# Column-tiled image transposes, a new order of weight loads and a new instruction order in a memory-recurrent attention kernel

## Chip, cores and metric

The kernel runs on one NeuronCore of a Trainium2 chip. The metric is device time of one execution in microseconds (us); several executions are timed, and one of them is profiled. All runs told here are of the ordinary ("fast") state, with a mean granted TensorE clock of 0.98 to 0.99. A ratio of two kernels is the mean time of one's fast runs over the mean of the other's fast runs of the same rounds on the same chip, so it isn't quite the ratio of the medians quoted beside it.

## The reference

Four layers alternate over 2048 tokens of width 512: A, B, A, B. Layer A is attention with a recurrent memory and decides the structure. Tokens come in 64 segments of 32; each segment is attended together with 8 memory rows, and the first 8 output rows become the memory of the next segment.

```python
for s in range(n_seg):                       # 64 segments, one after another
    xs = x[:, s * seg_len:(s + 1) * seg_len, :]
    h = jnp.concatenate([mem, xs], axis=1)   # 8 + 32 rows
    q = jnp.einsum('btd,dhe->bhte', h, Wq)   # 32 heads of 128; k and v likewise
    ...
    p = _softmax(jnp.where(mask, q @ k.T * scale, -1e9))
    o = jnp.einsum('bhte,hed->btd', p @ v, Wo)
    mem = o[:, :M, :]                        # the chain from segment to segment
    outs.append(o[:, M:, :])
```

Layer B is a linear attention over all tokens; its work is spread as filler over the segments of layer A. Wq, Wk, Wv and Wo have 4 MB each and stay in on-chip memory.

## The kernel before

The kernel is a list of nodes (a few instructions each, with the data they read and write) that a program orders on five engines before the launch. Each node has a priority: its step in the kernel plus a searched offset. Three parts matter here.

The loads of the weights. Nodes with smaller step plus offset go first; 13.5 is the length of a step, so with the old offsets Wv (-15.85) overtook Wk (4.75) and Wk overtook Wq (20.70), although the estimated landings belong to the order Wq, Wk, Wv:

```python
for i, (W, v, nm, t) in enumerate(((Wq_sb, qk_view[0], "Wq", 12.0), (Wk_sb, qk_view[1], "Wk", 21.0),
                                   (Wv_sb, qk_view[2], "Wv", 30.3))):
    P.at(-998 + i, "ld%d" % (2 + i))
    late.append(add("act", lambda a, W=W, v=v: a.dma_start(W[:, :, :], v), 0.5, writes=[nm], ..., lat=t))
# ... Wo: four quarters on SyncE; each waits for the load before the previous one
for i in range(4):
    nd = add("sp", lambda s, hs=hs: s.dma_start(Wo_sb[:, hs, :], ...), 0.9, ..., after=[late[-2]], ...)
    late.append(nd)
```

A projection of 32 rows fills only 32 columns of TensorE's array, so four of them run side by side in column tiles (`mode="col"`). The result, an "image", is copied out of PSUM (the memory that TensorE writes to) and, for queries and keys, must be turned. Of 640 images 256 are turned on TensorE and 384 by a DMA transpose. The latter are half of the images of each segment and all those of the "left blocks" (a segment has 40 rows; the 8 that do not fit into a block of 32 are gathered from four segments):

```python
def turned(W, key, blk, bkeys, b, dst, dkey, urgent, dma):
    tl = project(W, key, blk, bkeys, b, urgent)          # L753, mode="col"
    k = img_no[0] % NI if urgent else NI                  # one of few image buffers
    nd = evac(img[:, k, :], lambda: tl.f32()[:, :], 512, ..., writes=[("img", k)])   # L591 or L592
    if dma:
        add("sp", lambda e: e.dma_start_transpose(..., img[:, k, :]), 1.25, reads=[("img", k)], ...)   # L766
        return nd
    def tr(pe):                                           # L773
        for i in range(4):
            r = pe.transpose(tt.bf16()[:, 128 * i:128 * i + 128], img[:, k, 128 * i:128 * i + 128], id_sb[:, :])
        return r
    add("pe", tr, c_pe(4, 128), reads=[("img", k), "id"], tiles=[tt], urgent=urgent)   # mode "full"
    evac(dst..., 512, ...)
```

The ordering stays in the mode that TensorE is in (full array or column tiles) unless a node of the other mode is ahead by more than `MODE_SLACK` (`LOOK` is how far ahead, in us, it looks for a more urgent node before it fills in another):

```python
elif nd.prio < pick.prio - MODE_SLACK:
    break                       # the other mode is far more urgent: change
elif nd.mode == self.pe_mode:
    pick = nd                   # stay
```

Lines that the profiles name: L753 projections, L773 image transposes, L834 memory scores (L851, L864, L865: their sums and products), L889 and L800 scores in column tiles, L925 and L926 products with V, L949 output projection, L972 the hand-over of the memory to the next segment, L990 residual, L1085 and above layer B. In the changed kernel L773 is L775, and all lines below it are 3 higher (L834 is L837, L949 is L952, L972 is L975).

The softmax here doesn't subtract the row's maximum and nothing guards it: scores larger than these inputs give would overflow.

Of the kernel before, what the change touches and what calls it, by code (L numbers as in the profile page):

```python
# [16 lines left out]
HOP = 0.06  # L17
PE_SWITCH = 0.1
TURN = 1.8
MODE_SLACK = 26.39  # L20

LOOK = 0.000

PERIOD = 13.5
OFFSET = {
    "ld0": (-11.50,),
    "ld1": (4.90,),
    "ld2": (20.70,),
    "ld3": (4.75,),
    "ld4": (-15.85,),  # L30
    "startF": (-5.20,),
    "prepF": (4.30, 1.75, -2.15, 3.05, 7.55, 4.10, 2.90, -8.85, -8.80, 12.20, 4.50),
    "left0F": (-3.40, 1.15, -4.60, -5.90, 5.70, 0.00),
    "left1F": (-4.60, 1.35, -0.70, -0.35, 1.15, 5.25),
    "leftv0F": (30.85, -17.50),
    "leftv1F": (2.10, -15.75),
    "leftsF": (-4.25, 3.65, -1.55, 9.80),
    "xl": (16.05,),
    "qk0": (-19.20, -4.30, -2.55, -8.90, -4.20, 0.30),
    "qk1": (-1.75, 2.40, -4.40, 2.35, -6.40, -9.20, 11.50, -0.15),  # L40
    "v0": (0.30, 8.50),
    "v1": (4.55, 0.65),
    "mem0": (5.45, -0.45, -1.20, 0.55, 0.20, -2.10, 0.00, 1.25, -1.35),
    "mem1": (-10.80, -25.05, -8.05, 0.00, -0.65, -10.60, -14.15, 3.00, 0.60),
    "out": (-6.35, -2.55, -6.45, -3.20),
    "next": (0.50, -3.60, 0.10),
    "x": (3.45, 13.20, 11.25, -10.75, 6.60, -2.75, 26.25, -5.65, -0.15, -7.90, -8.10, -6.15, 7.95, -1.90,
        -5.05, -1.85, 6.35, 27.05, 19.50, 11.50, 27.45, 16.35, -0.50),
    "res": (28.65, 17.45, -1.00, -9.55, -0.60, -2.20, 2.25),
    "prep": (0.00, 11.35, 2.65, 5.95, -0.35, -1.00, 0.00, -3.10, 0.25, 1.85, -0.05),  # L50
    "left0": (3.25, -0.60, -3.40, -9.65, -2.20, 1.05),
    "left1": (34.80, -0.50, 7.70, 40.15, 13.10, -6.25),
    "leftv0": (0.00, 1.50),
    "leftv1": (42.50, 4.65),
    "lefts": (6.45, 0.40, 7.15, -4.05),
    "bi": (1.50, 4.25, -14.35, -1.70, 12.10, -1.15, -0.10, -3.45, 0.35, 17.45, 17.75, 0.10, 9.80, 16.90, 15.05,
        17.50, 7.80, 0.05, 0.60, -0.55, 4.90, -5.05, 5.75),
    "xL": (12.95, 3.75, 2.20, 1.30, -2.00, -0.25, -0.40, 8.00, -5.65, -2.10, -1.95, -0.20, -3.80, 0.00, -0.75,
        -0.90, -7.05, -34.30, -1.95, 5.75, 5.95, -3.00, -11.10),
    "outL": (1.90, 2.40, -2.95, -1.20),  # L60
    "resL": (0.30, 3.45, 0.10, -7.75, 13.20, -0.10, 11.75),
    "biL": (3.05, -3.75, -1.85, 3.75, 1.30, 0.50, -10.60, 8.80, -2.90, -1.80, -9.05, 0.45, 3.85, 0.95, -6.65,
        -8.45, 6.75, 2.00, 1.25, 0.00, 0.40, 0.25, 1.40),
    "bm": (6.85, 1.25, 3.45, -6.80, -5.20, 0.25, -0.75, -1.05, -3.05, -1.15, 2.25, 0.00, -10.65),
    "boF": (-15.85, -1.85, 18.50, 3.05, 3.25, 5.35, -0.85, -1.05),
    "bo": (5.15, 2.30, 10.70, -2.25, 1.05, -8.40, 18.75, -12.30),
    "boL": (1.20, 2.00, -2.55, -0.05, 8.50, 0.70, 0.35, -2.35, -6.40),
}


# [12 lines left out]
def c_pe(n_mm, n):  # L83
    return n_mm * max(0.0255, (n / 2.4 + 3.0) * 1e-3)
# [24 lines left out]
class _Prog:  # L109
# [27 lines left out]
    def add(self, engs, fn, cost, reads=(), writes=(), tiles=(), dsem=None, urgent=False, mode="full",  # L137
            after=(), lat=0.0):
        nd = _Node()
        nd.mode = mode  # L140
        nd.lat = lat
        nd.key = None
        if self.place is not None:
            step, name = self.place
            nd.key = (step, name, self.count)
            self.count += 1
        nd.soft = set()
        nd.engs = (engs,) if isinstance(engs, str) else tuple(engs)
        nd.cost = cost if isinstance(cost, dict) else {e: cost for e in nd.engs}
        nd.fn = fn  # L150
        nd.sync = set(after)
        nd.order = set()
        nd.tiles = tuple(tiles)
        nd.dsem = dsem
        nd.urgent = urgent
        nd.eng = nd.start = nd.done = nd.know = None
        nd.sig = False
        nd.val = 0
        nd.waits = []
        nd.idx = len(self.nodes)  # L160
        if dsem is not None:
            self.dma_tot[dsem] = self.dma_tot.get(dsem, 0) + 16
            nd.dval = self.dma_tot[dsem]
        for key in reads:
            st = self.res.setdefault(key, [None, []])
            if st[0] is not None:
                nd.sync.add(st[0])
            st[1].append(nd)
        for key in writes:
            st = self.res.setdefault(key, [None, []])  # L170
            if st[0] is not None and st[0] is not nd:
                nd.sync.add(st[0])
            for r in st[1]:
                if r is not nd:
                    nd.sync.add(r)
            st[0] = nd
            st[1] = []
        for tl in nd.tiles:
            if tl.ops:
                p = tl.ops[-1]  # L180
                if p.engs == ("pe",) and nd.engs == ("pe",):
                    nd.order.add(p)
                else:
                    nd.sync.add(p)
            tl.ops.append(nd)
        self.nodes.append(nd)
        return nd


    def schedule(self):  # L190
# [92 lines left out]
        def pick_for(e):  # L283
# [7 lines left out]
            while ready[e]:  # L291
# [17 lines left out]
                if pick is None:  # L309
# [3 lines left out]
                    held = item  # L313
                elif nd.prio < pick.prio - MODE_SLACK:
                    kept.append(item)
# [159 lines left out]
def _build_kernel(nc, A_x, A_mem0, A_Wq, A_Wk, A_Wv, A_Wo, A_seg_len, B_wqkv, B_wo, out):  # L475
# [26 lines left out]
    def sb(name, shape, dt=BF16):  # L502
        return E(nc.sbuf_tensor(name, shape, dt))

    Wq_sb = sb("Wq_sb", [128, 4, H * DH])
    Wk_sb = sb("Wk_sb", [128, 4, H * DH])
    Wv_sb = sb("Wv_sb", [128, 4, H * DH])
# [3 lines left out]
    id_sb = sb("id_sb", [128, 128])  # L511
# [34 lines left out]
    img = av((NI + 1) * 512).rearrange("p (r x) -> p r x", r=NI + 1)  # L546
# [38 lines left out]
    P = _Prog(nc, banks)  # L585
    add = P.add
# [17 lines left out]
    qk_view = [W.rearrange("(c p) h e -> p c (h e)", p=128) for W in (A_Wq, A_Wk, A_Wv)]  # L604
# [8 lines left out]

        return (t + shift[0]) % NX

    P.at(-1000, "ld0")
    add("sp", lambda s: s.dma_start(mem0_sb[0:M, :], A_mem0[0]), 0.1, writes=[MEM0], dsem="dmem", lat=2.0)
    P.at(-999, "ld1")
    add("sp", lambda s: s.dma_start(x_sb[:, 0, :], x_view[0]), 0.4, writes=[("x", 0)], dsem="dx0", lat=2.0)
    late = []  # L620
    for i, (W, v, nm, t) in enumerate(((Wq_sb, qk_view[0], "Wq", 12.0), (Wk_sb, qk_view[1], "Wk", 21.0),
                                       (Wv_sb, qk_view[2], "Wv", 30.3))):
        P.at(-998 + i, "ld%d" % (2 + i))
        late.append(add("act", lambda a, W=W, v=v: a.dma_start(W[:, :, :], v), 0.5, writes=[nm], dsem="d" + nm, lat=t))
    wo_view = A_Wo.rearrange("h e d -> e h d")
    P.at()
    for i in range(4):
        hs = slice(8 * i, 8 * i + 8)
        nd = add("sp", lambda s, hs=hs: s.dma_start(Wo_sb[:, hs, :], wo_view[:, hs, :]), 0.9, writes=[("Wo", i)],
                 dsem="dWo%d" % i, after=[late[-2]], lat=(12.4, 5.5, 5.6, 5.7)[i])  # L630
        late.append(nd)
    add("sp", lambda s: s.dma_start(wqkv_sb[:, :, :], B_wqkv.rearrange("(c p) f -> p c f", p=128)), 0.5,
        writes=["wqkv"], dsem="dwqkv", after=[late[-1]], lat=5.0)
# [38 lines left out]
    for j in range(4):  # L672
        q = slice(32 * j, 32 * j + 32)
        d = j % 2
# [3 lines left out]
        o = 16 + 224 * d + 96  # L678
        sel(scr_sb[q, o:o + 24], ALU.not_equal, 1.0, -8, [[-1, 24]], 1, *SCR)

        for g4 in range(4):
            o = 464 + 128 * d + 32 * g4 + 24
# [12 lines left out]
        reads=SCR, tiles=[tl])  # L695
# [42 lines left out]
    def a_layer(base, first):  # L738
# [20 lines left out]
        def turned(W, key, blk, bkeys, b, dst, dkey, urgent, dma):  # L759

            tl = project(W, key, blk, bkeys, b, urgent)
            k = img_no[0] % NI if urgent else NI
            img_no[0] += urgent
            nd = evac(img[:, k, :], lambda: tl.f32()[:, :], 512, tiles=[tl], writes=[("img", k)], urgent=urgent)
            if dma:
                add("sp", lambda e: e.dma_start_transpose(dst.rearrange("p h j x -> p h (j x)"), img[:, k, :]), 1.25,  # L766
                    reads=[("img", k)], writes=[dkey], dsem="turn%d" % k, lat=TURN)
                return nd
            tt = P.tile()

            def tr(pe):
                for i in range(4):
                    r = pe.transpose(tt.bf16()[:, 128 * i:128 * i + 128], img[:, k, 128 * i:128 * i + 128], id_sb[:, :])  # L773
                return r
            add("pe", tr, c_pe(4, 128), reads=[("img", k), "id"], tiles=[tt], urgent=urgent)  # L775
            evac(dst.rearrange("p h j x -> p (h j x)"), lambda: tt.bf16()[:, 0:512], 512, tiles=[tt], writes=[dkey],
                 rate=2, urgent=urgent)
            return nd
# [469 lines left out]
```

## Time and profile before

| | before |
|---|---|
| median of 3 runs | 1911.02 us (1909.57 to 1913.83) |
| span of the profiled run | 1907.5 us |
| TensorE busy | 93% |
| changes between full array and column tiles | 654 |
| first hand-over of memory | 67.4 us |
| 62 segments of the first layer A, hand-over to hand-over | 851.3 us |
| from the last of these to the first of the second layer A (the seam) | 65.0 us |
| 62 segments of the second layer A | 857.4 us |
| from the last hand-over to the end | 66.4 us |

The lower six rows are counted from the start times of TensorE's instructions; the last five add up to the span, so any gain must show in one of them.

### The profile page before, as it was taken

The page shows a single profiled execution, that of the slowest core. Times are in us where ns is not written, and L with a number is a line of the kernel's source. Part 1 is how long each engine was busy: PE and PEld are TensorE (multiplying, and loading weights), DVE is VectorE, ACT ScalarE, POOL GpSimd, SP SyncE. Part 2 cuts the span into 40 slices and gives each one's busy share as a digit, 9 for nine tenths or more (in the row PEclk, how much of TensorE's full clock was granted, in tenths as well). Part 3 has the DMA queues.
Part 4 walks back from the last instruction along what each step waited for, and adds up shares of the span by engine and source line. Part 5 has one row for each costly group of instructions (what it writes and reads, how often), then busy time and mean ns, then how long its engine had stood idle before and what let it go on. Part 6 is the DMA issues. An engine that isn't in the chain of part 4 may idle for free.

```text
span 1907.5 us, 88958 instructions
## 1 busy us (share of the span) xinstructions
PE 1780.8 (93%) x40739; PEld 1192.9 (63%) x40833; DVE 1092.2 (57%) x3242; ACT 1162.2 (61%) x3040; POOL 74.8 (4%) x172
## 2 busy tenths in 40 slices
PE   2899999999999999999789999999999999999986
PEld 0566666666666666666446666666666666666663
DVE  1356556656565656555545566666655666665655
ACT  1456666666666666666456666666666666666655
POOL 2000000000000000000000000000000000000000
PEclk9899999999999999999899999999999999999999
DMA  8611212212111222121121222222112122122213
GB/s 306 140 32 37 40 38 41 39 36 42 37 41 39 39 39 41 37 39 39 24 39 33 42 42 42 42 36 41 42 37 46 39 44 37 39 44 50 47 33 122
DMA packets 228231, 96.46 MB, mean 51 GB/s; under 512 B 211624, under 2 KB 222000, under 8 KB 226320
## 3 DMA queue, kind: packets, MB, share of 16 engines
q1 hardware_dynamic: 220656, 62.58, 18.2%
q0 software_dynamic: 5616, 15.60, 2.6%
q10 hardware_dynamic: 1584, 12.58, 1.6%
q8 instruction: 319, 5.23, 1.1%
q14 instruction: 56, 0.46, 0.1%
HBM read 29.89 MB, written 10.49 MB: 21 GB/s over the span
## 4 chain that ended last, share of the span: by engine, by line
PE 76%; DMA 16%; DVE 4%; ACT 3%; issue 1%; SPq 0%; ACTq 0%; DVEq 0%
PE pb L753 34%; PE pb L949 16%; DMA arena_sb<-arena_sb 13%; PE pb L1085 3%; PE pb L925 3%; PE pb L990 3%; PE pb L773 2%; PE pb L834 2%; ACT arena_sb L591 2%; PE pb L851 2%; PE pb L972 2%; PE pb L889 2%; DMA Wq_sb<-in_A_Wq_dram 2%; DVE arena_sb L592 2%; PE pb L1121 1%; PE pb L865 1%
## 5 line engine op out<-in xcount | busy, mean ns | idle before, releaser
L591 ACT ACTIVATE arena_sb<-pb 128x512 bf16<-128x512 f32 (+6 forms) x1287 | 667.3, 526 | 389.3 <-PE pb L753 326.0
L592 DVE CAST arena_sb<-pb 128x512 bf16<-128x512 f32 (+3 forms) x534 | 242.2, 456 | 353.9 <-PE pb L972 176.7
L753 PE MATMUL pb<-Wq_sb,arena_sb 128*32 128x512 bf16 x5120 | 354.0, 384 | 23.3 <-DMA Wq_sb<-in_A_Wq_dram 20.9
L753 PE MATMUL pb<-Wv_sb,arena_sb 128*32 128x512 bf16 x5120 | 318.7, 381 | 0.1
L949 PE MATMUL pb<-Wo_sb,arena_sb 128*32 128x256 bf16 x10368 | 314.5, 276 | 2.4 <-DVE arena_sb L868 1.8
L753 PE MATMUL pb<-Wk_sb,arena_sb 128*32 128x512 bf16 x5120 | 314.0, 380 | 0.0
L949 PEld LDWEIGHTS pb<-Wo_sb,arena_sb 128*32 128x32 bf16 x10368 | 269.8, 98 | 33.5 <-DVE arena_sb L868 22.8
L910 DVE TENSOR_TENSOR arena_sb<-arena_sb 32x256 bf16<-32x256 bf16 x512 | 212.9, 416 | 79.1 <-ACT arena_sb L906 67.2
L753 PEld LDWEIGHTS pb<-Wk_sb,arena_sb 128*32 128x32 bf16 x5120 | 138.7, 97 | 131.7 <-issue 1.2
L753 PEld LDWEIGHTS pb<-Wv_sb,arena_sb 128*32 128x32 bf16 x5120 | 138.5, 97 | 123.2 <-issue 1.8
L753 PEld LDWEIGHTS pb<-Wq_sb,arena_sb 128*32 128x32 bf16 x5120 | 123.5, 97 | 137.9 <-DMA Wq_sb<-in_A_Wq_dram 21.1
L591 ACT ACTIVATE outW_sb<-pb 128x128 fp32r<-128x128 f32 x257 | 71.4, 278 | 194.6 <-PE pb L949 191.6
L592 DVE COPY arena_sb<-pb 128x512 bf16<-128x512 bf16 (+2 forms) x265 | 97.7, 371 | 100.5 <-PE pb L773 77.7
L925 PE MATMUL pb<-arena_sb 128*128 128x128 bf16 x1024 | 128.6, 217 | 5.6 <-DVE arena_sb L912 5.5
L834 PE MATMUL pb<-arena_sb 128*128 128x32 bf16 x2016 | 112.5, 177 | 22.1 <-DMA arena_sb<-arena_sb 21.2
L912 DVE TENSOR_TENSOR arena_sb<-arena_sb 32x64 bf16<-32x64 bf16 x512 | 111.1, 217 | 15.9
L926 PE MATMUL pb<-arena_sb 128*128 128x32 bf16 x1024 | 118.1, 178 | 0.0
L841 ACT ACTIVATE arena_sb<-pb 128x256 bf16<-128x256 f32 x252 | 97.2, 386 | 29.0 <-PE pb L834 28.4
L868 DVE TENSOR_TENSOR arena_sb<-pb,arena_sb 128x128 bf16<-128x128 f32 x252 | 72.0, 290 | 64.8 <-ACT arena_sb L856 37.3
L834 PEld LDWEIGHTS pb<-arena_sb 128*128 128x128 bf16 x2016 | 86.9, 96 | 29.8 <-DMA arena_sb<-arena_sb 24.9
L773 PE MATMUL pb<-id_sb,arena_sb 128*128 128x128 bf16 x1024 | 95.7, 220 | 10.0 <-DVE arena_sb L592 5.6
L773 PEld LDWEIGHTS pb<-id_sb,arena_sb 128*128 128x128 bf16 x1024 | 58.4, 97 | 67.4 <-issue 30.1
(109 smaller groups left out, 2234.8 us busy)
## 6 DMA issues: line engine op xcount, KB each, us to landing
arena_sb<-arena_sb SPq DMA_TRANSPOSE x384, 2.5
Wv_sb<-in_A_Wv_dram ACTq DMA_DIRECT2D x1, 4096.0 KB, 13.6
Wk_sb<-in_A_Wk_dram ACTq DMA_DIRECT2D x1, 4096.0 KB, 23.7
Wq_sb<-in_A_Wq_dram ACTq DMA_DIRECT2D x1, 4096.0 KB, 33.0
Wo_sb<-in_A_Wo_dram SPq DMA_DIRECT2D x4, 1024.0 KB, 7.3
xs_scratch<-x_sb POOLq DMA_DIRECT2D x32, 128.0 KB, 2.0
pq_scratch<-arena_sb POOLq DMA_DIRECT2D x32, 128.0 KB, 2.3
x_sb<-xs_scratch POOLq DMA_DIRECT2D x16, 128.0 KB, 2.3
```

The costliest lines, as they stand in the source:

```text
L591: return e.activation(o() if callable(o) else o, i() if callable(i) else i, ACTF.Copy)
L592: return e.tensor_copy(o() if callable(o) else o, i() if callable(i) else i)
L753: r = pe.matmul(tl.f32()[32 * j:32 * j + 32, 0:512], blk[:, c, :], W[:, c, o:o + 512], start=(c == 0), stop=(c == 3), tile_position=(0, 32 ...
L773: r = pe.transpose(tt.bf16()[:, 128 * i:128 * i + 128], img[:, k, 128 * i:128 * i + 128], id_sb[:, :])
L834: r = pe.matmul(tl.f32()[:, o:o + 32], kk[:, hh, :, :].rearrange("p j x -> p (j x)"), qT[:, r2, hh, :, 0:8], start=True, stop=True)
L841: add("act", lambda a: a.activation(Pm[:, k, :, :].rearrange("p a q -> p (a q)"), tl.f32()[:, 0:256], ACTF.Exp, scale=SCALE), c_act(256), ...
L868: add("dve", lambda v: v.tensor_tensor(oTb[:, s % NO, 16 * b:16 * b + 16, 0:8], pv.f32()[:, 0:128].rearrange("p (n q) -> p n q", q=8), Rm[ ...
L910: add("dve", lambda v, q=q, j=j: v.tensor_tensor(Pbx[q, :, j, 0:32], Px[q, :, :], Rx[q, :, :], ALU.mult), c_dve(256) + 0.075, reads=["Px", ...
L912: add("dve", lambda v, q=q, j=j: v.tensor_tensor(Pbx[q, :, j, 32:40], PLL[q, g2, :, gl], Rx[q, :, 0:8], ALU.mult), c_dve(64) + 0.075, read ...
L925: pe.matmul(o, vimg[:, r2, e], Pbx[:, hh, :, 0:32], start=True, stop=False)
L926: return pe.matmul(o[:, :, 0:8], vleft[:, g2, e], Pbx[:, hh, :, 32:40], start=False, stop=True)
L949: r = pe.matmul(tl.f32()[32 * j:32 * j + 32, 0:256], oT[:, 4 * hh + n, :], Wo_sb[:, 8 * n + hh, 256 * d:256 * d + 256], start=(hh == 0 and ...
```

## The change

The intent: let the image transposes run in column tiles, so that they can stand among the projections without a change of mode; issue the weights in the order of their use; and search the order again for both. The diff, cut to its core:

```diff
-MODE_SLACK = 26.39
-LOOK = 0.000
+MODE_SLACK = 13.03
+LOOK = 0.073
 OFFSET = {
-    "ld2": (20.70,),
-    "ld3": (4.75,),
-    "ld4": (-15.85,),
+    "ld2": (2.50,),
+    "ld3": (-5.00,),
+    "ld4": (0.50,),
     ... (some 40 other rows, all new)
-        P.at(-998 + i, "ld%d" % (2 + i))
+        P.at(-9000 + 1000 * i, "ld%d" % (2 + i))
     ... (estimated landings of the weights, by 0.1 to 1 us)
             def tr(pe):
                 for i in range(4):
-                    r = pe.transpose(tt.bf16()[:, 128 * i:128 * i + 128], img[:, k, 128 * i:128 * i + 128], id_sb[:, :])
+                    for j in range(4):
+                        o = 128 * i + 32 * j
+                        r = pe.transpose(tt.bf16()[32 * j:32 * j + 32, 128 * i:128 * i + 128], img[:, k, o:o + 32],
+                                         id_sb[:, :], tile_position=(0, 32 * j))
                 return r
-            add("pe", tr, c_pe(4, 128), reads=[("img", k), "id"], tiles=[tt], urgent=urgent)
+            add("pe", tr, c_pe(4, 128), reads=[("img", k), "id"], tiles=[tt], urgent=urgent, mode="col")
```

## The prediction

> **What bounds the kernel now.** I read the page first (busy shares, slices), then the DMA issues of the first 70 us, then the timeline of TensorE at the start and in an ordinary segment, then the stretches. The page:
>
> ```profile
> PE 1780.8 (93%) x40739; PEld 1192.9 (63%) x40833; DVE 1092.2 (57%) x3242; ACT 1162.2 (61%) x3040; POOL 74.8 (4%) x172
> ...
> PE   2899999999999999999789999999999999999986
> ```
>
> TensorE is busy 93% while ScalarE and VectorE stay near 60%. Its slices fall below 9 in four places: the first two (0 to 95 us), the seam between the two layers and the end. So the kernel is a TensorE stream with a bad start. The start, as the DMA issues of the first 70 us give it (last column: us from issue to landing), then TensorE's timeline (start, duration, group, and in brackets the idle time before it and what ended that):
>
> ```profile
> Wv_sb<-in_A_Wv_dram ACTq DMA_DIRECT2D x1, 4096.0 KB, 13.6
> Wk_sb<-in_A_Wk_dram ACTq DMA_DIRECT2D x1, 4096.0 KB, 23.7
> Wq_sb<-in_A_Wq_dram ACTq DMA_DIRECT2D x1, 4096.0 KB, 33.0
> ```
>
> ```profile
> 34.89 5.26 PE L753 MATMUL pb<-Wq_sb,arena_sb 128*32 128x512 bf16 x48 [20.87 <-DMA Wq_sb<-in_A_Wq_dram]
> ...
> 64.94 1.93 PE L949 MATMUL pb<-Wo_sb,arena_sb 128*32 128x256 bf16 x64 [0.35 <-DMA Wo_sb<-in_A_Wo_dram]
> ```
>
> The three loads are issued at 0.8, 1.3 and 1.8 us in the order Wv, Wk, Wq and land at 14.4, 24.9 and 34.9. The first projection wants Wq, the last of them, so TensorE idles 20.9 us in one piece. The first output projection waits for Wo: its four quarters are issued on the SyncE queue at 40.4, 49.8, 52.9 and 56.9 us, because that queue works in order and has image transposes ahead of them that wait for Wq. The last quarter lands at 64.8. The first hand-over of memory to the next segment (L972) is at 67.4 us.
>
> An ordinary segment, TensorE's timeline:
>
> ```profile
> 903.23 1.93 PE L949 MATMUL pb<-Wo_sb,arena_sb 128*32 128x256 bf16 x64
> 904.98 0.42 PE L889 MATMUL pb<-arena_sb 128*32 128x32 bf16 x32
> ...
> 906.44 0.19 PE L902 MATMUL pb<-arena_sb,bo_sb 128*128 128x64 bf16 x1
> 906.56 1.05 PE L753 MATMUL pb<-Wq_sb,arena_sb 128*32 128x512 bf16 x16
> 907.43 1.90 PE L753 MATMUL pb<-Wk_sb,arena_sb 128*32 128x512 bf16 x32
> 909.16 1.04 PE L753 MATMUL pb<-Wq_sb,arena_sb 128*32 128x512 bf16 x16
> 910.02 1.90 PE L753 MATMUL pb<-Wv_sb,arena_sb 128*32 128x512 bf16 x32
> 911.86 0.40 PE L773 MATMUL pb<-id_sb,arena_sb 128*128 128x128 bf16 x4
> 912.33 0.27 PE L834 MATMUL pb<-arena_sb 128*128 128x32 bf16 x4
> 913.12 0.40 PE L773 MATMUL pb<-id_sb,arena_sb 128*128 128x128 bf16 x4 [0.53 <-DVE arena_sb L592]
> ```
>
> Durations contain pipeline latency, so I count starts. 32 projection matmuls take 909.16 - 907.43 = 1.73 us: eight packs of four column tiles, 0.216 us a pack. The output projection: 1.75 us for 16 packs, 0.109 each. After the last Wv pack (910.02 + 8 x 0.216 = 911.75) the transpose starts only at 911.86: that is a change from column tiles to the full array. Over the whole trace, counted so, 318 changes to full cost 97 ns and 305 back to columns 89 ns on average; 654 changes in all, 5.1 a segment (128 segments), some 61 us.
>
> Hand-overs (L972) come every 13.6 us (median). In the two steady stretches (67 to 880 and 970 to 1842 us, 1684 us) the matmuls' own start-to-start costs sum to about 1515 us; of the remaining 169 us some 57 are changes of mode, about 50 visible gaps (20 at L834, 7 at L773, 7 at L800), the rest small bubbles.
>
> **What the Trainium skill says.** "TensorEngine Tiling (Array Packing)", Key Properties: changing the tiling mode drains the engine. The 97 and 89 ns agree. "TensorE: Matmul & The Clock Gate", Part 3, The mechanism: tiles of one pack start about 4 ns apart and run together; here the tiles of a pack start 3 to 4 ns apart. Part 1 of that page: an idle array falls to half clock. At 34.89 us, 48 matmuls take 5.26 us where 12 packs at 0.216 would be 2.6, so it agrees. "DMA: Bandwidth & Descriptors", Queues, rings and completion order: an engine's hardware DMAs share one ring on each DMA engine, and descriptors start in order. The landings 10 us apart in order of issue agree.
>
> **The change, part by part.**
>
> (1) Order of weights. Wq, Wk, Wv should land at about 14, 25 and 35 us. TensorE can start the query projections at 14.5 instead of 34.9, the key projections at 25, and only values wait until 35. Twelve projections (six of segment 0, six of the left block) at 4 x 0.216 = 0.87 us are 10.4 us of stream; eight of them fit before 35. Then four value projections (3.5 us), probabilities and products follow, so segment 0 is ready for its output projection near 40 us, and Wo decides. The SyncE queue now meets transposes whose images exist early, so the first Wo quarter goes out when Wk lands (25), the second when Wv lands (35), the others as the first two land. 16.8 MB of weights at the 415 GB/s seen in the first 33 us need 41 us; with the chained issues (5.6 to 6 us each after 35) the last lands at 46 to 48. The first output projection then starts near 47 and the first hand-over at 49 to 50 instead of 67.4: 18 us. Two more left projections can be done while waiting (1.7 us); against that, the early segments may lack filling work. **I take 19 us.** It lasts to the end because what follows is TensorE-bound.
>
> (2) Transposes. 256 groups of four 128x128 transposes (56 ns each start to start, 0.22 us a group, 57 us in all) become 256 groups of sixteen with 32 columns of weights. The moving operand stays 128 wide, so a pack of four should stream in 53 to 56 ns, interpolated between L889 (N=32: 28 ns a pack) and L949 (N=256: 109 ns), both also loading weights for every matmul. **Cost unchanged**: four packs, 0.22 us; 6144 more instructions and loads, not a bound. The evacuations are untouched.
>
> What moves is the place: a transpose no longer has to wait for the full-array block. It can go among the projections as soon as its image is copied (0.60 us on ScalarE), and its own copy (0.42 us on VectorE) then runs under the Wv projections. So the 7 us of gaps at L773, part of the 20 at L834, and the latency from the end of the projections to the memory scores (about 1.2 us in the segment above, though mostly filled) shrink. The changes themselves: the full block after Wv is needed anyway for the scores, so no pair disappears with the transposes alone. Four a segment seem the least (projections, attention, output, hand-over), 512 against 654; perhaps half of the 142 surplus go: 71 x 0.093 = 6.6 us. Of about 50 us of gaps I give it 12. **About 18 us** in the steady stretches.
>
> (3) New order at the seam and the end: gaps of 14.5 us (880 to 970) and 19.5 us (1842 to the end) are chains of VectorE and DMA steps that the edit does not touch. **I give it 1 us.**
>
> Sum: 19 + 18 + 1 = 38; 1911 - 38 = **1873 us**.
>
> **Rivals.** (A) Start only: the segments were filled already (full blocks mix transposes with L925 and other work), so moving transposes gives nothing, and a new order has as much jitter as gain. For it: L773 gaps are 7 us of 1684. Time: about 1892. (B) The start is hidden: Wo's issue still sits behind transposes on SyncE, or early segments have nothing to fill their chain, so of 19 us only 8 remain. Against it: the waits before 64.9 all go back to Wq. Time: about 1884 with the rest as above. (C) Tiled transposes are dearer: weight loads not hidden, a pack 80 ns or more. 1024 packs x 25 ns = 26 us lost, time about 1899. Against it: the N=32 packs at 28 ns load weights just as often. (D) The shorter chain lets the search remove nearly all surplus changes and most gaps: 13 + 25 = 38 us in place of 18, time about 1853.
>
> **Range and chances.** A and B set the upper part, D the lower: 1857 to 1891 should hold it 8 times in 10. The 2% line is at 1873, my middle; the start alone can't reach it. Faster by over 2%: 0.47; within: 0.52; slower: 0.01.
>
> **What would show each step.** In the changed kernel's trace: Wq lands near 14 us, the first L753 starts near 14.5, and L972 first near 49 (step 1). Transposes (now 128*32, x16) stand among L753 groups with 0.21 to 0.23 us start to start; changes of mode fall from 654 toward 580; the median distance between hand-overs falls from 13.6 to about 13.45; gaps at L834 shrink (step 2). The seam and end keep their lengths (65.0 us between the hand-overs around the seam; 66 us from the last to the end). I would be wrong if the first Wo waits keep the first hand-over late, if a pack costs far from 56 ns, or if the search gained or lost elsewhere.

## More of the kernel before

The median of the kernel before moved between 1906.8 and 1912.0 us from round to round, so differences of a few us between kernels of different rounds are best read from the ratios.

Waits of TensorE in the kernel before, from the view of who waited for whom (total us, times, longest):

```profile
PE pb L834 <- DMA arena_sb<-arena_sb: 21.2, 39, 1.9
...
PE pb L773 <- DVE arena_sb L592: 5.6, 13, 0.7
PE pb L773 <- ACT arena_sb L591: 4.3, 12, 0.7
```

L834 waits for images turned by DMA; L773 waits for the copy of its image out of PSUM.

## The result, and the profile after

The changed kernel took 1868.36 us (median of 4 runs, 1865.94 to 1869.26) against 1910.42 us for the kernel before in the same rounds; the ratio is 0.9775 (95% interval 0.9758 to 0.9792). Repeated in later rounds it took 1867.66 us, and the ratio was 0.9795 (0.9775 to 0.9814). So it is some 2.0 to 2.3% faster. The page after:

```profile
PE 1762.9 (94%) x43796; PEld 1201.8 (64%) x43905; DVE 1065.5 (57%) x3267; ACT 1160.3 (62%) x3015; POOL 74.5 (4%) x172
...
PE   4899999999999999999799999999999999999996
```

TensorE is still the bound, and its first slice has changed most. Where the 40.0 us between the profiled spans come from:

| stretch | before | after | difference |
|---|---|---|---|
| to the first hand-over | 67.4 | 60.7 | -6.8 |
| first layer A, 62 segments | 851.3 | 831.3 | -20.0 |
| seam | 65.0 | 67.5 | +2.5 |
| second layer A, 62 segments | 857.4 | 841.5 | -15.9 |
| last hand-over to the end | 66.4 | 66.6 | +0.2 |

The gain in the segments is 35.9 us, twice what was predicted, and the start gives a third of what was predicted.

**The segments.** The changes of mode fell from 654 to 552, and within the two stretches of 62 segments from 610 to 512, that is 4.1 a segment. An ordinary stretch, the timeline of TensorE:

```profile
1109.26 0.40 PE L753 MATMUL pb<-Wv_sb,arena_sb 128*32 128x512 bf16 x4
1109.47 1.05 PE L753 MATMUL pb<-Wk_sb,arena_sb 128*32 128x512 bf16 x16
1110.33 0.41 PE L775 MATMUL pb<-id_sb,arena_sb 128*32 128x128 bf16 x16
1110.56 1.05 PE L753 MATMUL pb<-Wv_sb,arena_sb 128*32 128x512 bf16 x16
1111.42 0.41 PE L775 MATMUL pb<-id_sb,arena_sb 128*32 128x128 bf16 x16
1111.99 0.81 PE L1190 MATMUL pb<-arena_sb 128*128 128x512 bf16 x3 [0.16 <-issue]
1112.64 0.43 PE L837 MATMUL pb<-arena_sb 128*128 128x32 bf16 x11
```

The transposes follow the projections without a bubble (1109.47 to 1110.33 is 0.86 us, just four packs), a group takes 0.23 us from start to start, and the second group is the last column work before the full-array block. The full block then has layer B (L1190) and the memory scores (L837), and no transposes whose copies the scores wait for. The waits of TensorE show it too:

```profile
PE pb L775 <- ACT arena_sb L591: 20.2, 20, 7.1
...
PE pb L837 <- DMA arena_sb<-arena_sb: 2.5, 7, 0.8
```

The wait of the memory scores for DMA images fell from 21.2 to 2.5 us. The wait of the transposes rose from 9.9 to 24.0 us; 7.1 us of it is one wait in the start, but it rose within the two stretches too.

How much of the gain is gaps needs care: the two traces lack matmul records (the page above counts 43796 matmuls for 43905 weight loads, that of the kernel before 40739 for 40833), and a missing record looks like a gap. Counted as they are, the visible gaps within the two stretches fell from 47.7 to 34.9 us. Two later profiles are complete: e1 (the kernel before but for its first 70 us) and the changed kernel again. Between them the stretches shrink by 38.9 us and the gaps fall from 41.4 to 23.8 us (-17.6); 98 fewer changes at the 93 ns measured before make another 9.1. The remaining 12 us are delays too short to show as gaps. Most of them are in the full block: full-array matmuls over 128 and over 32 columns follow each other every 55 and 25 ns as a rule, and what they took beyond that fell from 27.7 to 10.9 us, most of all before the transposes (6.0 to 0) and the sums of the scores (L851, 6.7 to 1.6). The projections lost 5 us in the same way.

**The start.** TensorE's timeline:

```profile
14.38 4.04 PE L753 MATMUL pb<-Wq_sb,arena_sb 128*32 128x512 bf16 x48 [0.57 <-DMA Wq_sb<-in_A_Wq_dram]
19.13 0.41 PE L775 MATMUL pb<-id_sb,arena_sb 128*32 128x128 bf16 x16 [0.71 <-ACT arena_sb L591]
24.99 5.31 PE L753 MATMUL pb<-Wk_sb,arena_sb 128*32 128x512 bf16 x48 [5.46 <-DMA Wk_sb<-in_A_Wk_dram]
37.36 0.62 PE L775 MATMUL pb<-id_sb,arena_sb 128*32 128x128 bf16 x16 [7.06 <-ACT arena_sb L591]
...
57.16 2.90 PE L952 MATMUL pb<-Wo_sb,arena_sb 128*32 128x256 bf16 x64 [2.94 <-DMA Wo_sb<-in_A_Wo_dram]
```

The weights land as intended and the projections start at 14.4 and 25.0 us. But at 30.3 us TensorE stops for 7 us, for ScalarE. ScalarE in turn waits, as the timeline of all engines says:

```profile
33.66 1.08 ACT L591 ACTIVATE arena_sb<-pb 128x512 bf16<-128x512 f32 x2 [14.59 <-DMA arena_sb<-arena_sb]
```

It can't copy the next image because the image buffers are full, and they are full because the DMA transposes that should empty them are late. The DMA view of 17 to 33.5 us:

```profile
q10 hardware_dynamic: 806, 6.47, 98.1%
q1 hardware_dynamic: 605, 0.15, 4.5%
...
arena_sb<-arena_sb SPq DMA_TRANSPOSE x2, 17.5
```

The columns are packets, MB and share of the 16 DMA engines; q10 carries the weights. The two image transposes were issued at 16.95 and 18.32 us and landed at 33.58 and 36.63. In an undisturbed stretch (600 to 700 us) one takes 2.5 us:

```profile
q1 hardware_dynamic: 13056, 3.15, 18.7%
...
arena_sb<-arena_sb SPq DMA_TRANSPOSE x24, 2.5
```

They consist of some 544 packets each (13056 / 24), and beside the weights somewhat less than one small packet is served for each weight packet of 8 KB. The SyncE queue, which issues both the transposes and Wo:

```profile
24.96 0.39 SPq L629 DMA_DIRECT2D Wo_sb<-in_A_Wo_dram  x1
34.28 7.78 SPq L766 DMA_TRANSPOSE arena_sb<-arena_sb  x3
42.11 0.58 SPq L629 DMA_DIRECT2D Wo_sb<-in_A_Wo_dram  x1
```

The first Wo quarter, issued at 24.96, lands at 39.66. The second goes out only at 42.11, behind three transposes whose images could be copied only after 33.6; the last lands at 57.12. One wait (for Wq) was turned into another (for the image buffers).

### The profile page after: what moved, and what is told of

Same layout as the page of the kernel before. It is cut to its first block, busy times and chain, and to the rows that moved or that the text cites. A ratio compares the mean times of both kernels' runs of the same rounds, so it can differ in the third digit from the quotient of the medians.

```text
span 1867.5 us, 95161 instructions
## 1 busy us (share of the span) xinstructions
PE 1762.9 (94%) x43796; PEld 1201.8 (64%) x43905; DVE 1065.5 (57%) x3267; ACT 1160.3 (62%) x3015; POOL 74.5 (4%) x172
## 4 chain that ended last, share of the span: by engine, by line
PE 85%; DMA 10%; ACT 2%; DVE 2%; issue 1%; SPq 0%; ACTq 0%; DVEq 0%
PE pb L753 39%; PE pb L952 15%; DMA arena_sb<-arena_sb 8%; PE pb L928 4%; PE pb L837 3%; PE pb L775 3%; PE pb L993 3%; PE pb L1088 2%; PE pb L975 2%; PE pb L854 2%; PE pb L892 2%; PE pb L1124 1%; PE pb L868 1%; PE pb L1190 1%; PE pb L867 1%
## 5 line engine op out<-in xcount | busy, mean ns | idle before, releaser
L591 ACT ACTIVATE arena_sb<-pb 128x512 bf16<-128x512 f32 (+6 forms) x1309 | 682.0, 530 | 341.5 <-PE pb L753 272.5
L753 PE MATMUL pb<-Wk_sb,arena_sb 128*32 128x512 bf16 x5120 | 347.7, 383 | 5.5 <-DMA Wk_sb<-in_A_Wk_dram 5.5
L753 PE MATMUL pb<-Wv_sb,arena_sb 128*32 128x512 bf16 x5120 | 352.2, 381 | 0.0
L753 PE MATMUL pb<-Wq_sb,arena_sb 128*32 128x512 bf16 x5120 | 342.2, 383 | 5.4 <-DVE arena_sb L592 4.8
L952 PE MATMUL pb<-Wo_sb,arena_sb 128*32 128x256 bf16 x10368 | 312.3, 275 | 4.9 <-DMA Wo_sb<-in_A_Wo_dram 2.9
L592 DVE CAST arena_sb<-pb 128x128 bf16<-128x128 f32 (+3 forms) x452 | 179.9, 398 | 221.3 <-PE pb L975 110.0
L952 PEld LDWEIGHTS pb<-Wo_sb,arena_sb 128*32 128x32 bf16 x10368 | 274.2, 97 | 20.7 <-DMA Wo_sb<-in_A_Wo_dram 3.4
L592 DVE COPY arena_sb<-pb 128x512 bf16<-128x512 bf16 (+2 forms) x325 | 121.2, 380 | 191.6 <-PE pb L775 183.9
L775 PEld LDWEIGHTS pb<-id_sb,arena_sb 128*32 128x32 bf16 x4096 | 76.4, 96 | 95.0 <-ACT arena_sb L591 47.5
L775 PE MATMUL pb<-id_sb,arena_sb 128*32 128x128 bf16 x4096 | 103.1, 220 | 24.1 <-ACT arena_sb L591 20.2
L592 DVE CAST outW_sb<-pb 128x128 fp32r<-128x128 f32 x96 | 28.0, 292 | 161.6 <-ACT outW_sb L591 161.6
L929 PE MATMUL pb<-arena_sb 128*128 128x32 bf16 x1024 | 109.7, 178 | 0.0
L837 PE MATMUL pb<-arena_sb 128*128 128x32 bf16 x2016 | 89.3, 177 | 2.8 <-DMA arena_sb<-arena_sb 2.5
```

Of the source, the lines that this page charges most:

```text
L591: return e.activation(o() if callable(o) else o, i() if callable(i) else i, ACTF.Copy)
L592: return e.tensor_copy(o() if callable(o) else o, i() if callable(i) else i)
L753: r = pe.matmul(tl.f32()[32 * j:32 * j + 32, 0:512], blk[:, c, :], W[:, c, o:o + 512], start=(c == 0), stop=(c == 3), tile_position=(0, 32 ...
L775: r = pe.transpose(tt.bf16()[32 * j:32 * j + 32, 128 * i:128 * i + 128], img[:, k, o:o + 32], id_sb[:, :], tile_position=(0, 32 * j))
L837: r = pe.matmul(tl.f32()[:, o:o + 32], kk[:, hh, :, :].rearrange("p j x -> p (j x)"), qT[:, r2, hh, :, 0:8], start=True, stop=True)
L929: return pe.matmul(o[:, :, 0:8], vleft[:, g2, e], Pbx[:, hh, :, 32:40], start=False, stop=True)
```

## The experiments

Twelve runs followed: eleven edited kernels and the changed kernel again. The stretches below come from their profiled runs, cut at the hand-overs as above.

| run | median us | ratio to before | start | first A | seam | second A | end | changes |
|---|---|---|---|---|---|---|---|---|
| before | 1911.0 | 1 | 67.4 | 851.3 | 65.0 | 857.4 | 66.4 | 654 |
| changed kernel | 1868.4 | 0.9775 | 60.7 | 831.3 | 67.5 | 841.5 | 66.6 | 552 |
| e1 weights only | 1903.5 | 0.9967 | 60.5 | 851.3 | 66.0 | 860.1 | 68.6 | 654 |
| e2 tiles only | 2070.6 | 1.0839 | 67.5 | 940.8 | 66.3 | 927.8 | 67.6 | 1016 |
| e3 both, old priorities | 2066.6 | 1.0814 | 60.1 | 934.6 | 66.4 | 928.1 | 70.8 | 1016 |
| e4 changed, old weights | 1875.8 | 0.9817 | 67.3 | 829.7 | 67.2 | 843.0 | 66.2 | 552 |
| e5 changed, full transposes | 1893.6 | 0.9902 | 59.6 | 845.5 | 66.7 | 854.5 | 65.7 | 810 |
| e6 start on TensorE | 1870.6 | 0.9792 | 56.1 | 836.4 | 65.2 | 842.1 | 68.6 | 554 |
| e7 Wo on ScalarE's queue | 1876.2 | 0.9813 | 66.7 | 835.6 | 65.7 | 841.0 | 65.8 | 558 |
| e8 both of these | 1883.9 | 0.9850 | 68.1 | 837.0 | 65.8 | 842.7 | 65.9 | 554 |
| e9 unsearched, full | 1971.1 | 1.0332 | 65.2 | 879.8 | 66.5 | 888.7 | 70.5 | 796 |
| e10 unsearched, tiles | 1988.3 | 1.0426 | 68.3 | 889.8 | 67.3 | 889.7 | 70.5 | 906 |
| e11 mended start | 1867.9 | 0.9795 | 53.6 | 836.0 | 65.8 | 842.6 | 66.6 | 554 |
| changed kernel again | 1867.7 | 0.9795 | 60.7 | 831.2 | 67.0 | 841.3 | 65.6 | 552 |

### e1: the kernel before with the new order of weights

```diff
-    P.at(-998 + i, "ld%d" % (2 + i))
+    P.at(-9000 + 1000 * i, "ld%d" % (2 + i))
```

(with the new offsets and estimated landings of the five load nodes)

> The kernel before with the weights issued in the order Wq, Wk, Wv and nothing else (its order on the engines stays as it was but for a handful of rows in the first 60 us). Theory A (the start is worth what the first hand-over shows, 67.4 to 60.7 us): 4 to 9 us faster than before, about 1903. Rival of the prediction (the start is worth 19 us when its waits go): 1890 to 1894. First hand-over near 60 us under A, near 49 under the rival.

Measured: 1903.5 us, 0.33% or 6.3 us faster (95% interval 2 to 10 us). The first hand-over is at 60.5 us and the twelfth at 210.8 instead of 218.4, so the gain lasts. The waits are those of the changed kernel: two image transposes issued at 17.2 and 18.9 us land at 33.6 and 36.7, and TensorE waits 7.8 us. The prediction's 19 us for this part is refuted.

### e2 and e3: the tiled transposes under the old priorities

e2 is the kernel before with only the `tr` node of the diff changed, tiles and `mode="col"`; e3 has e1's edit as well.

> The kernel before with the column-tile transposes, marked as such for the ordering, old weight order and old priorities. Theory A (the gain in the segments needs both the tiles and priorities made for them): between 0 and 12 us faster than before, 1899 to 1911. Rival B (the tiles alone bring it, whatever the priorities): about 30 us faster, near 1880. Rival C (tiles are worth nothing, a new order is all): within 3 us of before.

> Both edits with the priorities of before. If the two are additive, the gain of this run is the sum of the gains of the two single edits within 3 us; what is left to the changed kernel (1868) is then the share of the new priorities. Theory A expects 1892 to 1905, so 24 us or more left to the new priorities; rival B expects 1872 to 1876.

Measured: 2070.6 and 2066.6 us, 8.4 and 8.1% slower than before. No theory had expected that. In the segments the changes rise from 610 to 976 and the visible gaps from 41 (e1's complete trace) to 124 us: 366 changes at 93 ns (34 us) and 83 us of gaps make 117 of the additional 160 us. The longest waits of e2 on TensorE:

```profile
PE pb L952 <- DVE arena_sb L871: 31.8, 50, 0.9
PE pb L975 <- ACT outW_sb L591: 24.0, 63, 0.4
```

The old priorities placed a transpose right behind the first scores. Marked as column work it has to wait there until TensorE leaves the full array, so the second scores, the output projection (L952) and the hand-over (L975) come late, and the full block is broken up. (The waits and changes are measured; that the rule about modes is what delays the transposes is read from the code and was not tested alone.) The weights gain about as much here as alone: by the medians e3 is 4 us faster than e2, and its first hand-over is 7.4 us earlier.

### e4: the changed kernel with the old order of weights

```diff
-    P.at(-9000 + 1000 * i, "ld%d" % (2 + i))
+    P.at(-7000 - 1000 * i, "ld%d" % (2 + i))
```

All engines but ScalarE keep their order row by row; on ScalarE only the three load issues change places.

> The changed kernel with its weights issued Wv, Wk, Wq again; every engine's order is otherwise the same, row by row. Theory A: 5 to 9 us slower than the changed kernel, 1873 to 1877, the loss all before the first hand-over. Rival of the prediction: 15 us or more slower, 1883 or above.

Measured: 1875.8 us, 7.4 us more than the changed kernel's median, with the first hand-over at 67.3 us and the segments unchanged, as theory A expected. Together with e1 this puts the weights at 6 to 7 us.

### e5: the changed kernel's order with full transposes

```diff
-                    for j in range(4):
-                        o = 128 * i + 32 * j
-                        r = pe.transpose(tt.bf16()[32 * j:32 * j + 32, 128 * i:128 * i + 128], img[:, k, o:o + 32],
-                                         id_sb[:, :], tile_position=(0, 32 * j))
+                    r = pe.transpose(tt.bf16()[:, 128 * i:128 * i + 128], img[:, k, 128 * i:128 * i + 128], id_sb[:, :])
```

The node stays marked as column work, so every other instruction keeps its place.

> The changed kernel with every instruction in its place, but each group of sixteen tiled transposes written as four 128x128 transposes again. A group that stands between column-tile work now costs two more changes of mode. In the changed kernel's trace some 130 to 145 of the 256 groups stand so. Theory D (a change of mode costs 0.19 us a pair wherever it is, and a tiled group costs what a full one does): 24 to 28 us slower than the changed kernel, about 1894. Rival C (the order is all, tiles are worth nothing): within 5 us of the changed kernel. Rival E (tiled transposes are dearer than full ones): under 15 us slower.

Measured: 1893.6 us, 25.2 us more than the changed kernel's median (24.4 between the profiled spans). There are 810 changes, 258 more: 129 of the 256 groups stood between column work, and each change costs 24.4 us / 258 = 95 ns (within the two stretches alone, 27.2 us / 248 = 110 ns). Theory D holds. The timeline shows both changes around one such group:

```profile
1111.44 0.39 PE L753 MATMUL pb<-Wv_sb,arena_sb 128*32 128x512 bf16 x4
1111.77 0.40 PE L773 MATMUL pb<-id_sb,arena_sb 128*128 128x128 bf16 x4
1112.09 1.05 PE L753 MATMUL pb<-Wv_sb,arena_sb 128*32 128x512 bf16 x16
```

From the pack at 1111.44 to the transposes it is 0.33 us where a pack takes 0.216, and from there to the next projections 0.32 us where the tiled group took 0.23. So 0.2 us go per group. Rival C (only the order matters) and rival E (tiled transposes are dearer) are refuted: a tiled group costs what a full one does, and it pays where it stands among column work.

Compared with e1 (old order, full transposes, the same weights), e5 is 0.65% faster, some 12 us (7 to 17 by the two intervals), although it has 156 more changes. Its visible gaps in the stretches are 23.1 us, as in the changed kernel (23.8) and not as in e1 (41.4). So the new order removes the gaps in either form of the transposes, and the tiles spare the changes that this order would cost without them. So the path from before to the changed kernel, in this sequence of steps, is: weights 6 us, order 12 us, tiles 20 to 25 us. In another sequence the shares differ, as e2 shows.

### e6, e7, e8: what holds the start

e6 sends the images of segment 0 and of the first left block through TensorE instead of the DMA; e7 issues the four Wo loads on ScalarE's queue right behind Wv; e8 does both. In all three, TensorE's order is the changed kernel's again from about 94 us of its trace on, shortly before the fourth hand-over; before that it differs. (The diff leaves out priority rows for the moved nodes and the estimated landings of Wo.)

```diff
+                pe_only = first and s == 0 and b == 0          # e6, e8; likewise for the left block of tile 0
-                turned(Wq_sb, "Wq", blk, bk, b, qT[...], ("qT", r2, b), True, QDMA[b])
+                turned(Wq_sb, "Wq", blk, bk, b, qT[...], ("qT", r2, b), True, QDMA[b] and not pe_only)
...
-        nd = add("sp", lambda s, hs=hs: s.dma_start(Wo_sb[:, hs, :], ...), 0.9, ..., after=[late[-2]], ...)
+        nd = add("act", lambda s, hs=hs: s.dma_start(Wo_sb[:, hs, :], ...), 0.5, ...)      # e7, e8: no chain
```

> The changed kernel, but the six images of segment 0 and of the first left block that go through DMA transposes go through TensorE as well; from about row 200 on TensorE's order is the same. Theory F (in the changed kernel the image transposes issued at 17 us land only at 33.6 because the weight loads keep the DMA engines busy, the image buffers stay full, and that holds TensorE, the SyncE queue and so Wo): first hand-over between 49 and 54 us in place of 60.7, total 1857 to 1862. Rival G (Wo's chained issue on SyncE holds the start by itself): first hand-over at 58 or later, total within 3 us of the changed kernel.

> The changed kernel with the four Wo loads issued on the ScalarE queue right behind Wv instead of in a chain on SyncE; image transposes stay on DMA. Rival G: first hand-over near 50 us, total 1857 to 1862. Theory F: Wo lands by 47, but the image transposes now starve until all weights are in (44 to 47 us), so the first hand-over is at 60 or later and the total is the changed kernel's or up to 8 us more.

> Both of the last two edits. The weights land by 46 us and nothing else stands before the first output projection: first hand-over 48 to 51 us, total 1855 to 1860, which would beat both kernels. If early segments lack work to fill their chains (prediction's rival B), the hand-over moves but the total gains less than two thirds of it.

e6 removes the 7 us wait: theory F is right about what held TensorE at 30 us. The first hand-over comes at 56.1 us, short of the 49 to 54 expected, because Wo still lands only at 52.3. But the total is 1870.6 us, no gain. The hand-overs of e6 are ahead of those in the changed kernel's first profile by 4.6, 2.1, 1.1 and 0.5 us (first to fourth), and later within a microsecond or two of them. (In the changed kernel's second profile the second hand-over comes 1.5 us earlier, so the early ones vary by that much.) Its timeline has the reasons:

```profile
52.36 3.20 PE L959 MATMUL pb<-Wo_sb,arena_sb 128*32 128x256 bf16 x64 [4.37 <-DMA Wo_sb<-in_A_Wo_dram]
...
64.20 0.36 PE L844 MATMUL pb<-arena_sb 128*128 128x32 bf16 x8 [1.78 <-DMA arena_sb<-arena_sb]
...
68.34 3.61 PE L959 MATMUL pb<-Wo_sb,arena_sb 128*32 128x256 bf16 x64 [0.31 <-DVE arena_sb L878]
```

The output projections at 52.4 and 68.3 us take 3.2 and 3.6 us instead of 1.93: the granted clock is 0.5 from 51.6 to 55.0 and from 65.3 to 72.1 us, around and after the waits of 4.4 and 1.8 us. In between, the image transposes of segment 1 meet the loads for layer B.

e7 and e8 say nothing about their theories, since they broke something else. ScalarE's timeline in e7:

```profile
2.39 35.26 ACTq L630 DMA_DIRECT2D Wo_sb<-in_A_Wo_dram  x4
37.68 1.28 ACT L591 ACT_TABLE_LOAD   x1 [37.68 <-issue]
```

Issuing four more loads behind 12.6 MB of weights held ScalarE until 37.7 us, so it did no layer norm and no copies. The first projections came after 42 us, the first hand-overs at 66.7 and 68.1. Both kernels are slower than the changed one, and the expectation for e8 (1855 to 1860) failed with them.

### e9 and e10: without any searched priorities

Both use the longest remaining chain as the priority (`OFFSET = {}`), the new weight order, `MODE_SLACK` 13.03 and `LOOK` 0.073. They differ in the `tr` node alone.

> No searched priorities at all (longest remaining chain first), new weight order, full-array transposes. It is the base for the next run. Expected well slower than both kernels, 2000 to 2300 us, with over 700 changes of mode.

> The same with tiled transposes counted as column work; nothing else differs. Theory H (the tile form is a gain by itself and the priorities of before were merely made for the other form): 10 to 60 us faster than the run with full transposes, with some 100 to 250 fewer changes. Rival I (the tile form only pays under an order searched for it): within 10 us of that run, or slower.

Measured: 1971.1 and 1988.3 us; with tiles it is 0.9% slower, with 110 more changes. (e9 itself came out below the 2000 to 2300 expected.) Rival I holds: the tile form isn't a gain by itself.

### e11: the mended start

Besides e6's edit, the four Wo loads are issued on SyncE in two pairs, behind Wk and behind Wv, and the loads for layer B are put off to segment 2.

```diff
-                 dsem="dWo%d" % i, after=[late[-2]], lat=(12.4, 5.6, 5.7, 5.8)[i])
+                 dsem="dWo%d" % i, after=[late[(-2, -3, -3, -4)[i]]], lat=(13.4, 15, 10, 12)[i])
...
+            if first and s == 2:
+                late.append(P.nodes[-1])
+                load_wqkv()
+                load_wo_b(1)
```

> The changed kernel with the images of segment 0 and the first left block on TensorE, the four Wo loads issued in two pairs (behind Wk and behind Wv), and the loads for the second kind of layer put off to segment 2, so that they no longer meet the image transposes of segment 1. TensorE's order is the changed kernel's from about row 200 on. If the start's waits are what the gain was lost to: first hand-over 48 to 53 us, the fifth near 104 (111.1 in the changed kernel), total 1858 to 1863. If early segments are bound by their own chain and half clock: fifth hand-over at 108 or later, total 1865 or more.

> The changed kernel itself on the same chip as the run with the mended start: 1866 to 1870 us.

Measured: 1867.9 us against 1867.7 for the changed kernel on the same chip, both 0.9795 of before. No version beats the changed kernel. Wo landed at 49.3 us and the first hand-over came at 53.6, the second at 65.8: 7.1 us ahead of the changed kernel of the same chip. By the fourth 2.0 us were left. Most of the loss is in one interval (16.1 us where the changed kernel takes 11.9):

```profile
88.19 0.41 PE L779 MATMUL pb<-id_sb,arena_sb 128*32 128x128 bf16 x16 [2.89 <-ACT arena_sb L594]
91.56 2.96 PE L960 MATMUL pb<-Wo_sb,arena_sb 128*32 128x256 bf16 x64 [0.37 <-DVE arena_sb L879]
```

The load for layer B, issued at 79.1 and landed at 86.9, now met the image transposes of segment 3 (issued at 81.4 and 82.7, landed at 87.5 and 87.9). TensorE waited 2.9 us, and the next output projection ran mostly at half clock (0.5 granted from 90.3 to 93.7 us), 1.0 us longer than 1.93. That is 3.9 of the 4.2 us lost in this interval; as TensorE's order differs from the changed kernel's up to here, the order is a rival for the rest. So the collision was moved, not removed. The fifth hand-over, at 107.5, lies between the two forecasts; the total fits the second.

## Why the prediction was right in its sum and wrong in its parts

The time (1873 predicted, 1868.4 measured) lies well inside the range. Two terms of the sum were mis-sized in opposite directions, and that they cancelled was luck.

- **The start, 19 us: it was 6 to 7** (e1 and e4). The landings of Wq, Wk and Wv were right to about a microsecond. The step that failed is "the second when Wv lands (35), the others as the first two land". The first Wo quarter did go out when Wk landed (24.96), but the DMA transposes of the early images took 17 to 18 us beside the weights instead of 2.5. So the image buffers stayed full, TensorE stopped for 7 us, later transposes went ahead of the second quarter in the SyncE queue, and it was issued at 42.11; Wo landed at 57.1, not at 46 to 48. I had named rival B with 8 us remaining for a start held by Wo, and spoke against it because all waits before 64.9 us went back to Wq. That was the error: the removal of a wait shows what stands behind it only when one follows the other resources of that time, here DMA engines that were full until 36 us.
- **"It lasts to the end because what follows is TensorE-bound."** True for the 7 us of e1 and e4. Not true for what e6 and e11 gained beyond: most of that was given back by the fourth hand-over, and e6 and e11 show waits for DMA images and half clock after them. What little is lost later stays open.
- **Transposes at unchanged cost: right.** A group takes 0.23 us against 0.22 (e5 confirms it from the other side). Its working was loose: a straight line between 28 ns (N=32) and 109 ns (N=256) gives 63 ns for a pack, not 53 to 56; the trace shows 55 to 56.
- **The steady stretches, 18 us: they were 36.** "Perhaps half of the 142 surplus" changes was the mis-sized term: 102 went, 98 of them in the segments. By the prediction's own account (changes and visible gaps) the complete traces show 9.1 + 17.6 = 27 us against 6.6 + 12 predicted; 12 us more went in short delays that the prediction had listed as "the rest small bubbles" and given nothing. The prediction's rival D came closest with 38 us, but its parts (13 + 25) were not the measured ones either. (The prediction's 318 + 305 changes are those without an idle gap before them; the other 31 of the 654 have one.)
- **"No pair disappears with the transposes alone": right, and too mild.** Alone the tiles add pairs (e2, e10). With an order made for them they save 258 changes against the same order with full transposes (e5). The prediction counted the changes that existed in the old order; it didn't count those that a better order would have cost without the tiles.
- **Seam and end, 1 us: they gave none.** The seam became 2.5 us longer, the end stayed. The seam varies between 65.0 and 67.5 us over the runs, and I made no experiment on it.

The prediction's rivals A (only the start) and C (dear tiles) are refuted by e5. How far a new search with full transposes could have come isn't known: e5's order was searched for tiles, so its 12 us over e1 are no upper bound.

## What to carry to other kernels

When an engine has modes that cost a drain, put an operation into the mode of its neighbours and then order anew: under the old order the same edit cost 8%. Judge it by an exchange in place (same order, other form), which separates the form from the order. When a load is moved forward, look at what shares the DMA engines at that moment: small transfers that used to be quick can become the next wait.

## What the Trainium skill lacked or had wrong

- "TensorEngine Tiling (Array Packing)", Key Properties, says that a change of tiling mode drains the engine and gives no size. Here it was 97 ns into the full array and 89 ns back, and 95 to 110 ns each as the price of the additional changes in e5.
- "DMA: Bandwidth & Descriptors", Queues, rings and completion order, says that the DMA engines go round between queues packet by packet. It doesn't say what this does to a DMA transpose, which is made of small packets: 544 of them for one image of 128x512 took 2.5 us alone and 16.6 us beside 8 KB weight packets, with 605 small and 806 large packets served between 17 and 33.5 us.
- No page that I read says that issuing loads can hold the issuing engine for tens of us: four loads of 1 MB behind three of 4 MB held ScalarE for 35.3 us (e7), while in the kernel before one such load took 0.4 to 0.6 us to issue on SyncE. Why isn't shown.
- "TensorE: Matmul & The Clock Gate", Part 4, gives about 275 ns for a 128x128 bf16 transpose in a kernel's context. Here the median recorded duration of one (L773) is 219 ns, and back to back they start every 56 ns.
